# Thirty rows for every score and maxima product, with zero rows under the low parts, in a gated mix of local and full attention

## The chip, the core and the metric

The kernel runs on one core of one Trainium2 chip. The metric is the device time of one execution in microseconds (us); lower is better. The core has five engines that run side by side and wait for each other through semaphores: TensorE (PE; PEld is its weight load), VectorE (DVE), ScalarE (ACT), GpSimd (POOL) and SyncE (SP, which here issues nearly all DMAs).

## What is computed

For one sequence of S = 2048 positions with D = 448 features, 16 heads of 28 features each:

```python
x = A_x
g = _sigmoid((x * gate_w).sum(-1, keepdims=True))
a = _A_ref(x, A_wqkv, A_wo)   # each position looks at itself and 7 earlier ones, 2 apart
b = _B_ref(x, B_wqkv, B_wo)   # full attention over all positions, no mask
return g * a + (1 - g) * b
```

Both branches project x to queries, keys and values, take scores q.k times 28 ** -0.5, a softmax, the weighted sum of the values, and an output projection. All data are float32.

## The kernel before

**Precision.** A float32 operand is split into a high part, rounded to the format that TensorE takes in one pass (F32R), and a low part, the rest. A product of two such operands is the sum of three terms: high x high, high x low, low x high. The queries and keys of branch B go through DRAM as `qk_hi` and `qk_lo`.

**Tiles with four heads.** A key tile (`KH` high, `KL` low) has 128 rows: head h of a group of four sits in rows 32h to 32h+27. There are 4 such groups (g), and 4 blocks of 512 queries (b), so 16 units u = 4g + b. Rows 28 and 29 of each head have a special use in the first term: `KH` is filled with 1.0 before its keys are loaded (`init_kh`, L83), so these two rows stay 1.0, and rows 28 and 29 of the high query tile `QH` hold minus the row maximum of the scores, as a high and a low part (`load_nm`). So the first term, taken over 30 rows, yields the score minus the maximum. The two other terms take 28 rows.

**Projections (to about 248 us).** A list of tiles is worked through in order: the tiles of queries and keys of B, then values, then branch A. For each, TensorE multiplies (L320, L325), ScalarE, VectorE and GpSimd split and store. Between them TensorE already takes the first score maxima of B: `s1_mm` (L149) multiplies high queries (`QP`, two pairs of tiles in turn) and high keys, and VectorE reduces to the maximum (L171). In this part the maxima products take 64 rows, two heads at a time with the other one's query rows zero.

**Attention (from about 248 to 820 us).** 256 steps: for each unit, 16 key tiles of 128. In a step, `scores` issues 12 score products (4 heads x 3 terms, L1042) into three pairs of PSUM banks, and up to three maxima products for a later unit (L149, into T), in the order of the list `WITH` (`10 20 s0 11 21 30 00 ...`: head, then term; s for a maxima product), or `ALONE` when no maxima are left. Each product has 512 columns and stands in the row group of 32 rows of its head. ScalarE takes the exponential of two heads at once (L1047), VectorE the maxima (L155), and TensorE then multiplies the exponentials with the values (`av`, L1008). At the same time GpSimd and VectorE work through branch A from lists, with costs and due times that set which item is issued in which step. The query tiles of the next unit are loaded in step 12 of a unit (`load_q`, `load_part`): `QH` and `QL` come from a pool with two buffers each.

**End (from 820 us).** The output projection of both branches (L886).

**Fills.** At the start GpSimd fills `KH[0]` and `KH[1]` with 1.0 (L83), and VectorE fills a zero tile `t0` (L212) and two small ones. The third key tile `KH[2]` and the second low-key tile `KL[1]` get their memory when the projections' memory is free, in `main_tiles` in the first step of the attention stage; `KH[2]` is filled there, and then a mask (L620, L625). Keys are loaded later: into `KH[1]` behind tile 22, into `KL[0]` behind tile 62, into `KL[1]` in step 30. The order of instructions on each engine is the order in which the program issues them.

Of the kernel before, what the change touches and what calls it, by code (L numbers as in the profile page):

```python
# [8 lines left out]
F32 = mybir.dt.float32  # L9
F32R = mybir.dt.float32r  # L10
# [5 lines left out]
S, D, H, DH = 2048, 448, 16, 28  # L16
NB, NJ, NG = 4, 16, 4
W, DIL = 8, 2
HALO = (W - 1) * DIL
SCALE = DH ** -0.5  # L20
NU = NG * NB
NMX = 192
# [3 lines left out]
def gated_mix_kernel(ctx: ExitStack, tc: tile.TileContext, xT, xn, gw, wA, wB, woAB, out):  # L26
    nc = tc.nc
# [47 lines left out]

    QP = [[cp.tile([128, 512], F32R, name=f"QP{i}{k}") for k in range(2)] for i in range(2)]

    def init_kh(t):
        nc.gpsimd.memset(t.bitcast(F32), 1.0)  # L83

    def pair(name):
        return pp.tile([128, 2, 512], F32, tag="P", name=name)
# [18 lines left out]
            r = D + 112 * g + DH * h  # L105
            dma_r(t[32 * h:32 * h + DH, c], src[r:r + DH, c])

    def load_part(u, name, src):
        g, b = divmod(u, NB)
        t = sp.tile([128, 512], F32R, name=name)  # L110
        for h in range(4):
            r = 112 * g + DH * h
            dma_r(t[32 * h:32 * h + DH, :], src[r:r + DH, 512 * b:512 * b + 512])
        return t
# [1 line left out]
    Qs = {}  # L116

    def load_q(u, low=True):
        Qs[u] = load_part(u, "QH", qk_hi), load_part(u, "QL", qk_lo)
        if low:  # L120
            load_nm(u)

# [18 lines left out]
    def s1_mm(n, bank, half=False):  # L141
        u, i = divmod(n, 64)
        qs, kc, h = i // 16, i // 4 % 4, i % 4
        if u == 0:
            qs, kc = i // 8 % 4, 2 * (i // 32) + i // 4 % 2
        if i == 0 and u + 1 < NU:
            load_qhi(u + 1)
        r = slice(64 * (h // 2), 64 * (h // 2) + 64) if half else slice(32 * h, 32 * h + DH)
        nc.tensor.matmul(bank, qhis[u][h % 2][r, 128 * qs:128 * qs + 128],  # L149
                         KH[u // NB % 3][r, 512 * kc:512 * kc + 512], start=True, stop=True)  # L150

# [54 lines left out]
            nc.sync.dma_start(nm[u].bitcast(F32)[:, 32 * a:32 * a + 32], r[32 * a:32 * a + 32, :])  # L206


    for t in KH:
        init_kh(t)  # L210
    t0 = pair("t0")[:, 0, :]
    nc.vector.memset(t0, 0.0)  # L212
    nc.vector.memset(zt, 0.0)
    nc.vector.memset(omt, 0.0)

    zero = nc.const_aps.tensor(0.0, [128, 512], F32).bitcast(F32R)

# [8 lines left out]
    if True:  # L226
# [259 lines left out]
        for n, t in enumerate(tiles[:-1]):  # L486
            wi = t[0]
            for w in loads:
                if loads[w] == n:
                    load_w(w)  # L490
            for w in splits:
                i, k = (n - splits[w][0]) * splits[w][1], splits[w][1]
                if 0 <= i < 4:
                    split_w(w, range(i, i + k))
            if n in (3, 5):
                split_x((n + 1) // 2)
            if n < FULL:
                project(n)
            else:
                project_halves(n, [S1_START <= m < S1_START + 80 for m in (n, n + 1)])  # L500
            if n == 0:
                split_x(1, (3,))
            if t[1] == "qk":
                for m in {0: (), 1: (0, 1)}.get(n, (n,)):
                    qk_tile(m, *tiles[m][2:4])
            elif t[1] == "v":
                add_halves(n, V[:, t[2], :, 0:DH])
            else:
                a_tile(n, t[2], t[3])
            if n == 1:  # L510
                split_x(1, range(3))
            if n == 4:
                for t in QP[1]:
                    nc.scalar.activation(t, t0, AF.Copy)
            while fini and fini[0][0] <= n:
                fini.pop(0)[1]()
            if n == 2:
                load_w(1, (False,))
            if n == 3:
                load_qhi(0)  # L520
            if n in (3, 8):
                load_k(0, KH[0], qk_hi, slice(0, 1024) if n == 3 else slice(1024, S))
            if n == 3:
                load_w(1, (True,))
            if n == 16:
                for i in (1, 2):
                    nc.sync.dma_start(a_scr[i][:, 0:NJ, :].rearrange("c j e -> c (j e)").rearrange(
                        "c (a b) -> c a b", b=NJ), omg[0:8, None, :].to_broadcast([8, 56, NJ]))
            if n == 32:
                nc.gpsimd.memset(V[:, :, :, DH:], 1.0)  # L530
            if n == 22:
                load_k(1, KH[1], qk_hi)
            if n == 62:
                load_k(0, KL[0], qk_lo)
            if parts and parts[0][0] <= n:
                _, u, t = parts.pop(0)
                max_store(u, max_turn(t))
            if finished and n < len(tiles) - 3:
                u = finished.pop(0)
                parts.append((n + 3, u, max_parts(u)))  # L540
            if n == 64:
                gate = []
                for sgn, dst in ((-1.0, g_t), (1.0, omg)):
                    e = sp.tile([128, NJ], F32, name="ez")
                    nc.scalar.activation(e, zt, AF.Exp, scale=sgn)
                    nc.gpsimd.tensor_tensor(out=e, in0=e, in1=V[:, 0, :, DH], op=ALU.add)
                    gate.append((dst, e))
            if n in (66, 68):
                nc.vector.reciprocal(*gate.pop(0))
            if n == 70:  # L550
                r = sp.tile([128, 32], F32, name="omr")
                nc.vector.transpose(r, omt)
                for a in range(4):
                    nc.sync.dma_start(og_scr.rearrange("(j p) -> j p", j=NJ)[:, 32 * a:32 * a + 32],
                                      r[32 * a:32 * a + NJ, :])
            if n == 76:
                load_q(0)
# [51 lines left out]
    def main_tiles():  # L609
        nonlocal mp, pm, maskt, actx, a1, a2, a3  # L610
        hctx.close()
        mp = ctx.enter_context(tc.tile_pool(name="mp", bufs=1))

        KH.append(mp.tile([128, S], F32R, name="KH2"))
        KL.append(mp.tile([128, S], F32R, name="KL1"))
        init_kh(KH[2])
        pm = ctx.enter_context(tc.tile_pool(name="pm", bufs=8))

        maskt = mp.tile([128, W, NJ, 2], F32, name="maskt")
        nc.gpsimd.memset(maskt, 0.0)  # L620
        for st, g, t, src in ((12, 2, KH[2], qk_hi), (30, 1, KL[1], qk_lo), (72, 2, KL[0], qk_lo),
                              (100, 3, KH[0], qk_hi), (136, 3, KL[1], qk_lo)):
            at("end", st, lambda g=g, t=t, src=src: load_k(g, t, src))
        for w in range(1, W):
            nc.gpsimd.memset(maskt[0:1, w, 0:DIL * w, :], -1e9 / SCALE)  # L625

        actx = ExitStack()
        a1 = actx.enter_context(tc.tile_pool(name="a1", bufs=1))
        a2 = actx.enter_context(tc.tile_pool(name="a2", bufs=2))
        a3 = actx.enter_context(tc.tile_pool(name="a3", bufs=5))  # L630
        for nme in ("k", "v"):
            for i in range(2):
                t = a1.tile([128, HALO + NJ, 56], F32, name=f"{nme}t{i}")
                kvt[nme, i] = t
# [384 lines left out]
    def scores(u, kt, cur):  # L1019
# [9 lines left out]
        for tok in WITH if k else ALONE:  # L1029
            if tok[0] == "s":  # L1030
                i = int(tok[1])
                if i < k:
                    s1_mm(n + i, bank[tok])
                if i == 0:
                    s1_max(n, 1, T1)
                elif i == 2 and k > 1:
                    s1_max(n + 1, k - 1, other[:, 0:k - 1, :])
                continue
            a, t = tok[0], int(tok[1])
            h = (int(a) + n) % 4  # L1040
            r = slice(32 * h, 32 * h + (DH + 2 if t == 0 else DH))
            nc.tensor.matmul(bank[a], (KH[g % 3], KH[g % 3], KL[g % 2])[t][r, ks], (qh, ql, qh)[t][r, :], start=(t == 0), stop=(t == 2))  # L1042
            if t == 2 and a in "20":
                if len(exps) < 5:
                    probs.append(pair("P"))
                p = probs[len(exps) % 5]
                e = nc.scalar.activation(p, one if a == "2" else mine, AF.Exp, scale=SCALE).ins  # L1047
                for o in exps[-5:-4]:
                    tc.declare_no_dep(e, o, query=mybir.DependencyQuery.ANY_SYNC,
                                      reason="PE has read what it wrote, and this one waits for PE")  # L1050
                for o in maxs[-4:]:
                    tc.declare_no_dep(e, o, reason="PE waited for it and the exponential waits for PE")
                exps.append(e)
                cur[(h + 3) % 4], cur[h] = p[:, 0, :], p[:, 1, :]
                yield len(cur)
# [86 lines left out]
```

## Time and profile before

| | us |
|---|---|
| median of 3 runs | 896.78 (896.74 to 896.83) |
| the profiled execution | 896.69 |
| its span, first to last instruction | 894.9 |
| TensorE busy | 890.2 |
| VectorE busy | 740.5 |
| ScalarE busy | 642.4 |
| GpSimd busy | 638.7 |

The span is the time between the first and the last instruction of the profiled execution; the execution's own time has some 1.8 us around it. A busy engine is one with an instruction in flight; products of TensorE are pipelined and their ends are modelled, so starts tell more than ends. In a group's line stand line, engine, operation, output and inputs, shape, count, the busy time in all, and the mean duration in ns; behind it, in brackets or behind a bar, is the idle time before and what ended it.

### The profile page before, as it was taken

What the parts mean: (1) busy time and instruction counts of PE and PEld (TensorE: products, weight loads), DVE (VectorE), ACT (ScalarE), POOL (GpSimd) and SP (SyncE); (2) the same over time, 40 slices, a digit from 0 to 9 for tenths busy, and PEclk for the clock granted to TensorE, in tenths of its full rate; (3) what the DMA queues carried; (4) which work ended last, traced back from release to release, by engine and by line L of the source; (5) the groups of instructions that cost most, each with busy time, mean ns of one, the idle gap of its engine ahead of it and who ended that gap; (6) DMA issues with size and microseconds to landing.
All of it is one profiled execution on the core that took longest, in us unless ns stands there. A gap on an engine that the chain in (4) does not pass through costs nothing.

```text
span 894.9 us, 20516 instructions
## 1 busy us (share of the span) xinstructions
PE 890.2 (99%) x8312; PEld 533.4 (60%) x8312; DVE 740.5 (83%) x962; ACT 642.4 (72%) x766; POOL 638.7 (71%) x505
## 2 busy tenths in 40 slices
PE   9999999999999999999999999999999999999998
PEld 7889999999954444444444444444444444434997
DVE  6688999999979999999999999999999999832220
ACT  7456434343378898898988989989888898897220
POOL 1499846464459789998999989999999799701000
PEclk9999999999999999999999999999999999999999
DMA  8886403454372241225225222533121322437781
GB/s 267 277 267 186 151 12 84 135 142 121 103 248 66 89 139 46 67 61 156 71 56 143 86 62 86 128 96 98 45 64 32 89 43 49 104 78 214 192 265 52
DMA packets 114038, 104.51 MB, mean 117 GB/s; under 512 B 75240, under 2 KB 82280, under 8 KB 113160
## 3 DMA queue, kind: packets, MB, share of 16 engines
q1 hardware_dynamic: 113512, 102.42, 40.7%
q8 instruction: 65, 1.06, 0.5%
q10 hardware_dynamic: 432, 0.79, 0.3%
q14 instruction: 29, 0.24, 0.1%
HBM read 62.20 MB, written 40.96 MB: 115 GB/s over the span
## 4 chain that ended last, share of the span: by engine, by line
PE 99%; ACT 0%; issue 0%; ACTq 0%
PE T L1042 31%; PE av L1008 28%; PE r L325 15%; PE r L320 8%; PE T L886 8%; PE r L149 4%; PE T L149 4%; PE r L220 0%; PE av L472 0%; ACT P L1047 0%; ACT res L895 0%; ACT onhi L943 0%; ACT L L679 0%; ACTq L943 0%
## 5 line engine op out<-in xcount | busy, mean ns | idle before, releaser
L1047 ACT ACTIVATE P<-T 128x1024 f32<-128x1024 f32 x512 | 496.8, 1023 | 59.6 <-PE T L1042 57.9
L155 DVE TENSOR_REDUCE MX<-T 128x1 f32<-128x512 f32 x470 | 442.5, 954 | 31.7 <-PE T L149 13.7
L1008 PE MATMUL av<-P,V 128*32 128x512 f32 x2048 | 272.7, 605 | 0.0
L1042 PEld LDWEIGHTS T<-QH,KH 30*128 30x128 f32 x1024 | 92.2, 181 | 229.1 <-ACT P L1047 196.5
L149 PE MATMUL T<-KH,QP 28*128 28x512 f32 x704 | 220.3, 456 | 0.1
L1042 PE MATMUL T<-QH,KH 30*128 30x512 f32 x1024 | 211.7, 489 | 0.2 <-ACT P L1047 0.2
L171 DVE TENSOR_REDUCE MX<-r 128x2 f32<-128x1024 f32 x160 | 192.9, 1221 | 20.1 <-PE r L149 16.3
L1042 PE MATMUL T<-QH,KL 28*128 28x512 f32 x1024 | 185.7, 393 | 0.0
L1042 PE MATMUL T<-QL,KH 28*128 28x512 f32 x1024 | 184.3, 392 | 0.0
L653 POOL TENSOR_TENSOR prod<-qt,kt 128x896 f32<-128x896 f32 x64 | 135.4, 2116 | 6.4 <-DMA kt<-a_scr 6.4
L397 ACT ACTIVATE raw<-r 128x896 f32<-128x896 f32 (+1 forms) x62 | 57.1, 921 | 94.5 <-PE r L325 91.9
L149 PE MATMUL r<-KH,QP 64*128 64x512 f32 x320 | 114.5, 391 | 0.0
L714 POOL TENSOR_TENSOR oat<-oat,prod 128x896 f32<-128x896 f32 x48 | 101.2, 2109 | 2.0
L149 PEld LDWEIGHTS T<-KH,QP 28*128 28x128 f32 x704 | 86.1, 181 | 26.7 <-ACT P L1047 17.7
L325 PE MATMUL r<-wh,xh 64*128 64x448 f32 (+1 forms) x504 | 99.6, 363 | 0.0
L709 POOL TENSOR_TENSOR prod<-vt,L 128x896 f32<-128x896 f32 x56 | 95.3, 1702 | 0.3
L398 POOL TENSOR_TENSOR ast<-raw 128x448 f32<-128x448 f32 x47 | 54.3, 1154 | 56.4 <-ACT raw L397 43.9
L1042 PEld LDWEIGHTS T<-QL,KH 28*128 28x128 f32 x1024 | 94.3, 185 | 0.0
L1042 PEld LDWEIGHTS T<-QH,KL 28*128 28x128 f32 x1024 | 93.3, 183 | 0.2
L1008 PEld LDWEIGHTS av<-P,V 128*32 128x32 f32 x2048 | 40.3, 107 | 77.9 <-issue 65.4
L325 PE MATMUL r<-wl,xh 64*128 64x448 f32 (+1 forms) x441 | 79.0, 365 | 0.0
L325 PEld LDWEIGHTS r<-wh,xh 64*128 64x128 f32 x504 | 77.9, 185 | 0.1
(122 smaller groups left out, 1138.8 us busy)
## 6 DMA issues: line engine op xcount, KB each, us to landing
a_scr<-ast SPq DMA_DIRECT2D x24, 448.0 KB
qk_hi<-qkh SPq DMA_DIRECT2D x24, 256.0 KB
qk_lo<-qkh SPq DMA_DIRECT2D x24, 256.0 KB
rbc<-rs SPq DMA_DIRECT2D x64, 64.0 KB
QP<-qk_hi SPq DMA_DIRECT2D x64, 56.0 KB
KL<-qk_lo SPq DMA_DIRECT2D x16, 224.0 KB
QH<-qk_hi SPq DMA_DIRECT2D x64, 56.0 KB
QL<-qk_lo SPq DMA_DIRECT2D x64, 56.0 KB
```

The lines of the kernel that those rows point to most:

```text
L149: nc.tensor.matmul(bank, qhis[u][h % 2][r, 128 * qs:128 * qs + 128], KH[u // NB % 3][r, 512 * kc:512 * kc + 512], start=True, stop=True)
L155: i = nc.vector.tensor_reduce(MX[:, n % NMX:n % NMX + k], bank, axis=X, op=ALU.max)
L171: nc.vector.tensor_reduce(m, PM[k], axis=X, op=ALU.max)
L320: nc.tensor.matmul(bank, ws[c][rows, k, t[4]:t[4] + 128], x, start=first, stop=last)
L325: nc.tensor.matmul(bank[:, 0:cols], x, ws[c][rows, k, 0:cols], start=first, stop=last)
L653: nc.gpsimd.tensor_tensor(out=p, in0=qt[c], in1=kvt["k", c % 2][:, HALO - DIL * w:HALO - DIL * w + NJ, :], op=ALU.mult)
L709: nc.gpsimd.tensor_tensor(out=dst.rearrange("p j (h d) -> p j h d", d=DH), in0=kvt["v", c % 2][:, HALO - DIL * w:HALO - DIL * w + NJ, :].r ...
L714: nc.gpsimd.tensor_tensor(out=ows[c % 2][:, :, 0:56] if w == W - 1 else oat[c], in0=oat[c], in1=oat[c, w], op=ALU.add)
L886: writes(bank, nc.tensor.matmul(bank[:, :D], src, wo[c][k], start=(first and k == ks[0] and i == 0), stop=(last and k == ks[-1] and i == 2)))
L1008: nc.tensor.matmul(av[32 * h:32 * h + 32, :], V[:, kt, 4 * g + h, :], tiles_[h], start=(kt == 0), stop=(kt == NJ - 1), skip_group_check=True)
L1042: nc.tensor.matmul(bank[a], (KH[g % 3], KH[g % 3], KL[g % 2])[t][r, ks], (qh, ql, qh)[t][r, :], start=(t == 0), stop=(t == 2))
L1047: e = nc.scalar.activation(p, one if a == "2" else mine, AF.Exp, scale=SCALE).ins
```

## The change

Every score product and every maxima product of the attention stage takes 30 rows. For this the low query tiles `QL` become two fixed tiles, filled with zeros by VectorE at the start, and used in turn; the low key tiles are filled with zeros before their keys are loaded. So rows 28 and 29 are zero in one of the two operands of the second and the third term, and zero in the queries of a maxima product. `KH[1]` is filled in the program behind the fifth entry of the tile list (n == 4) and no longer at the very start, and `KL[0]` with it, both by GpSimd; `KL[1]` is filled by GpSimd in `main_tiles`, behind `KH[2]` and ahead of the mask.

```diff
+ROWS = DH + 2
...
+    QL = [cp.tile([128, 512], F32R, name=f"QL{i}") for i in range(2)]
...
+    def init_kl(t):
+        nc.gpsimd.memset(t.bitcast(F32), 0.0)
...
-    def load_part(u, name, src):
+    def load_part(u, t, src):
         g, b = divmod(u, NB)
-        t = sp.tile([128, 512], F32R, name=name)
...
-        Qs[u] = load_part(u, "QH", qk_hi), load_part(u, "QL", qk_lo)
+        Qs[u] = load_part(u, sp.tile([128, 512], F32R, name="QH"), qk_hi), load_part(u, QL[u % 2], qk_lo)
...
-        r = slice(64 * (h // 2), 64 * (h // 2) + 64) if half else slice(32 * h, 32 * h + DH)
+        r = slice(64 * (h // 2), 64 * (h // 2) + 64) if half else slice(32 * h, 32 * h + ROWS)
...
-    for t in KH:
-        init_kh(t)
+    init_kh(KH[0])
     t0 = pair("t0")[:, 0, :]
     nc.vector.memset(t0, 0.0)
     nc.vector.memset(zt, 0.0)
     nc.vector.memset(omt, 0.0)
+    for t in QL:
+        nc.vector.memset(t.bitcast(F32), 0.0)
...
             if n == 4:
                 for t in QP[1]:
                     nc.scalar.activation(t, t0, AF.Copy)
+                init_kh(KH[1])
+                init_kl(KL[0])
...
         init_kh(KH[2])
+        init_kl(KL[1])
...
-            r = slice(32 * h, 32 * h + (DH + 2 if t == 0 else DH))
+            r = slice(32 * h, 32 * h + ROWS)
```

## The prediction

> **What bounds the kernel now.** I read the page first, for the engine that the end hangs on; then the table of windows, to split the span into stages; then single steps of the attention stage in order of time; then the two source lines whose products the change touches; last the start of the span and the start of the attention stage, where the fills stand.
>
> ```profile
> span 894.9 us, 20516 instructions
> PE 890.2 (99%) x8312; PEld 533.4 (60%) x8312; DVE 740.5 (83%) x962; ACT 642.4 (72%) x766; POOL 638.7 (71%) x505
> PE 99%; ACT 0%; issue 0%; ACTq 0%
> PE T L1042 31%; PE av L1008 28%; PE r L325 15%; PE r L320 8%; PE T L886 8%; PE r L149 4%; PE T L149 4%; PE r L220 0%; PE av L472 0%; ACT P L1047 0%; ACT res L895 0%; ACT onhi L943 0%; ACT L L679 0%; ACTq L943 0%
> ```
>
> ```profile
> core 0: us, PE busy (x) PEld busy (x) DVE busy (x) ACT busy (x) POOL busy (x), PEclk, DMA share, GB/s
> 248.00:820.00 572.00, 571.73 (x5822) 238.37 (x5820) 514.37 (x735) 511.12 (x572) 488.08 (x350) 1.00 0.34 92
> ```
>
> The chain that ended last is TensorE from end to end, and the products that the change widens (L1042, and L149 into T) are 35% of it. The attention stage fills about 572 of the 894.9 us. It is 256 steps (16 units of 16 key tiles), so a step is about 572 / 256 = 2.23 us. TensorE is busy in all of it at a granted clock of 1.00, with ScalarE (511.12) and VectorE (514.37) at 90%. Full busy does not yet mean that TensorE streams all the time, so I looked into two steps. The lines give start, duration, and how many products were merged.
>
> ```profile
> 382.86 0.50 PE L1042 MATMUL T<-QH,KH 30*128 30x512 f32 x2
> 382.87 0.50 PE L149 MATMUL T<-KH,QP 28*128 28x512 f32 x1
> 383.08 0.49 PE L1042 MATMUL T<-QH,KH 30*128 30x512 f32 x1
> 383.20 0.40 PE L1042 MATMUL T<-QL,KH 28*128 28x512 f32 x2
> 383.21 0.39 PE L1042 MATMUL T<-QH,KH 30*128 30x512 f32 x1
> 383.42 0.39 PE L1042 MATMUL T<-QL,KH 28*128 28x512 f32 x1
> 383.43 0.39 PE L1042 MATMUL T<-QH,KL 28*128 28x512 f32 x1
> 383.44 0.39 PE L1042 MATMUL T<-QL,KH 28*128 28x512 f32 x1
> 383.44 0.60 PE L1042 MATMUL T<-QH,KL 28*128 28x512 f32 x2
> 383.66 0.41 PE L149 MATMUL T<-KH,QP 28*128 28x512 f32 x2
> 384.00 1.06 PE L1008 MATMUL av<-P,V 128*32 128x512 f32 x8
> 385.00 0.50 PE L1042 MATMUL T<-QH,KH 30*128 30x512 f32 x2
> ...
> 385.39 0.50 PE L1042 MATMUL T<-QH,KH 30*128 30x512 f32 x2
> 385.56 0.40 PE L1042 MATMUL T<-QH,KL 28*128 28x512 f32 x2
> ...
> 387.30 0.50 PE L1042 MATMUL T<-QH,KH 30*128 30x512 f32 x2
> ```
>
> A step holds 15 products of 512 columns in four row groups of 32, one for each head, which run side by side; so in one row group there are at most four in a row. In a row group the products follow each other every 0.23 us (383.20 to 383.43, 383.21 to 383.44). The first of a step takes 0.11 more, because its weight load is not hidden: 382.86 to 383.20 is 0.34. The first of these two steps takes 2.14 us (382.86 to 385.00), the second 2.30 (385.00 to 387.30); in the second the last two high products start only at 385.39, with the long duration, because their PSUM pair was still being read. So TensorE streams back to back but for such waits of about a tenth of a step. Whatever a wider product costs in streaming would show in the time in full; whatever only shortens a wait gains a few tenths of a microsecond in a step at most.
>
> **Part 1: rows 28 to 30.** Two of the three terms of a score (2 x 1,024 products) and the maxima products of this stage (704) get two more rows; that is 2,752 instructions and none more than before. Two more zero rows leave the sums as they are. The price is that of two rows in a product of 512 columns.
>
> ```profile
> engine op xcount: duration ns min/median/max, first and last start us, forms
> L1042 PE MATMUL T<-QH,KH x1024: 387/494/503, 248.4 to 819.5; 30*128 30x512 f32 x171
> L1042 PE MATMUL T<-QL,KH x1024: 384/392/417, 248.8 to 819.8; 28*128 28x512 f32 x171
> L1042 PE MATMUL T<-QH,KL x1024: 382/392/498, 249.0 to 820.1; 28*128 28x512 f32 x171
> L149 PE MATMUL T<-KH,QP x704: 382/489/505, 248.5 to 778.0; 28*128 28x512 f32 x176
> L149 PE MATMUL r<-KH,QP x320: 385/392/398, 32.0 to 245.5; 64*128 64x512 f32 x160
> ```
>
> These are minimum, median and longest duration in ns. At first sight 30 rows cost 494 and 28 rows 392. But the maxima products have 28 rows and a median of 489, and 64 rows take 392. The two values are a product whose weight load is hidden (382 to 398) and one whose load is not (about 490), in every shape. Which of the two it is hangs on what the product waited for: the 30-row product at 383.21 followed a 28-row one in its row group and took 0.39, the 28-row ones at 382.87 and 30-row ones at 382.86 opened a step and took 0.50 alike.
>
> Now the ends. The shortest 30-row product, 387, is 3 to 5 ns above the shortest 28-row ones, 384 and 382. Four run side by side, so 2,752 products are 688 in sequence, and 688 x 3 to 5 ns is 2.1 to 3.4 us more. The other end is the 64-row form against the longest of the hidden 28-row medians: 392 against 392 is 0, and from the shortest 64-row one, 385, to the 387 of 30 rows it is 2 ns less for more rows, 688 x 2 ns = 1.4 us less. I take 0: the distance between starts is the price in a stream, and it is 0.23 us behind a 30-row product (383.21 to 383.44) as behind a 28-row one (383.20 to 383.43).
>
> No new wait comes with the two rows. The second term reads rows of the key tile that the first term of the same head has read already; the third term reads the query rows with the maxima, which the first term of that head has waited for. The low query tiles stay two in turn, as they were in their pool, and their loads keep the same 28 rows, size and place in SyncE's queue.
>
> **Part 2: the fills.** At the start VectorE gets two fills of 128x512, GpSimd keeps the fills of the first two key tiles and gets one of 128x2048 for the low keys.
>
> ```profile
> 1.25 3.54 POOL L83 MEMSET KH<- 128x2048 f32 x2
> 30.26 1.03 POOL L235 TENSOR_TENSOR wl<-raw,wh 128x384 fp32r<-128x384 f32 x1 [25.47 <-ACT wh L234]
> 0.91 0.48 DVE L212 MEMSET t<- 128x512 f32 x1 [0.91 <-PEq L1134]
> 4.64 0.43 DVE L443 CAST xh<-V 128x512 fp32r<-128x512 f32 x1 [3.18 <-DMA V<-in_xT]
> 5.22 0.71 PE L320 MATMUL r<-xh,wh 128*128 128x512 f32 x2
> L862 DVE CAST oahi<-oar 128x512 fp32r<-128x512 f32 x3 | 1.3, 429 | 10.8 <-DMA oar<-oa_scr 10.8
> ```
>
> VectorE: 2 x 0.48 = 0.96 us, in the 3.18 us in which it waits for the first input; cost 0, and up to 0.96 if that cover were gone. GpSimd: in its own order there is nothing between the first key fill and the place behind four tiles, and the new fills wait for nothing, so I expect all three one behind the other at the start, ending near 4.79 + 1.8 = 6.6 us. The next thing GpSimd does is at 30.26, after 25.47 us of waiting. The first loads into those tiles are issued behind tile 22 and tile 62, long after. Cost 0; even if the fills were to wait for the fourth tile they would fit into the same gap.
>
> At the start of the attention stage GpSimd gets one more fill, for the second low-key tile, behind that of the third key tile.
>
> ```profile
> 252.50 1.81 POOL L83 MEMSET KH<- 128x2048 f32 x1 [1.86 <-PE av L472]
> 254.24 0.31 POOL L620 MEMSET maskt<- 128x256 f32 x1
> 254.95 0.21 POOL L192 TENSOR_TENSOR nmt<-nmv,nmt 128x16 fp32r<-128x16 f32 x1
> 261.60 2.13 POOL L653 TENSOR_TENSOR prod<-qt,kt 128x896 f32<-128x896 f32 x1 [6.44 <-DMA kt<-a_scr]
> 259.25 0.20 DVE L201 STREAM_TRANSPOSE nms<-nmt 128x32 f32<-128x32 f32 x1
> ```
>
> It takes 254.24 - 252.50 = 1.74 us of GpSimd's order. Behind it stand the mask fills and the low part of the maxima, which goes from 254.95 to about 256.7; VectorE's transpose of it starts at 259.25, still 2.3 us later. The first product waits for a load until 261.60 and keeps 6.44 - 1.74 = 4.7 us of slack. Cost 0; without that cover 1.74 us on GpSimd, which stands nowhere in the chain. The load of that tile, at step 30, is 30 x 2.23 = 67 us away.
>
> **The sum.** 0 + 0 + 0 against the profiled execution's 896.69 us (span 894.9 and 1.8 around it), which is 0.09 below the median of 896.78. Forecast: 896.8 us, no change that can be told: about 0.2%, or 1.8 us, is what a measurement of this kernel can tell from none.
>
> **Rivals.** *Slower: a lock at the start.* If the third fill holds VectorE off, the cast at 4.64 starts when that fill ends: 4.79 + 1.74 = 6.53, so 1.89 us later, and the first real products at 5.22 wait for that cast. TensorE has no slack to give it back: 898.7. It decides if the fill gets in before the cast, that is if the first input lands after about 4.73. Against it: the cast began 0.15 us before the second fill ended and took 0.43, as the casts of the same shape in line L862 took 0.429 on average; but 0.15 is little overlap, and GpSimd's ends are rough. [...]
>
> *Slower: two rows cost streaming time.* With the 3 to 5 ns above: 898.9 to 900.2. With the whole difference of the medians, 102 ns in 688, 70 us: 967, against which the 28-row products at 0.50 and the 30-row one at 0.39 speak outright.
>
> *Faster: mixed row counts were what kept weight loads from hiding.* Then the late pair of the 385.00 step would lose its 0.11 us, and with it every step: 256 x 0.11 = 28 us, 868.6. For it: most 30-row products have the long duration. Against it: low query products always follow a 30-row product in their row group, and their longest is 417; the maxima products at the end of a step follow a 28-row one, and more than half have the long duration.
>
> *It does not do what it says:* the fills run at the start and not behind four tiles, as said in part 2; that changes nothing in the sum.
>
> **How the numbers follow.** No change on the path: 0.77. Lock at the start: 0.07; streaming price of two rows: 0.08; faster by hidden loads or a better fit of the waits: 0.08. So faster 0.08, same 0.77, slower 0.15. The range goes down to the lower end of part 1 (896.8 - 1.4 = 895.4) and up to the first end of the streaming price (898.9), which takes in the lock; left out are the 28 us gain and the rest of the slow cases.
>
> **What the profile after would show.** Right: all T products of L1042 and L149 as 30x512, with shortest durations of 382 to 387 and 0.23 us from one to the next in a row group; steps of 2.14 to 2.30 us; three fills at the start, GpSimd's next work still near 30.3; the cast of L443 at 4.6 and the first real product at 5.2; GpSimd's first product still waiting for its load near 261.6. Wrong: a cast that starts at 6.5; a 0.24 us distance in a row group; low query products with durations near 490; a stage of attention that is more than 2 us longer or shorter than 572.

## The result, and the profile after

| | before | after |
|---|---|---|
| median of 16 runs, us | 896.81 | 898.61 |
| lowest to highest, us | 896.40 to 897.81 | 897.12 to 899.79 |
| the profiled execution, us | 896.69 | 898.69 |
| its span, us | 894.9 | 896.9 |

The ratio is 1.0015, with a 95% interval of 1.0008 to 1.0022: slower, by 1.3 us by the ratio and 1.8 by the medians, clear of no change at all and just about at the 0.2% up to which the prediction spoke of none. The result lies inside the stated range (895.4 to 898.9). But the three zeros of the sum are not what happened: the start cost about 3 us in the profiled execution and the attention stage gave 0.9 back. The runs after also spread more than those before, in three groups: five near 897.2, ten near 898.6 and one at 899.8.

The start of the changed kernel in order of time, VectorE, GpSimd, then TensorE (start, duration, what, in brackets the idle time before and what ended it):

```profile
1.52 1.02 DVE L219 MEMSET QL<- 128x512 f32 x2
4.65 2.17 DVE L448 CAST xh<-V 128x512 fp32r<-128x512 f32 x1 [2.11 <-DMA V<-in_xT]
6.86 0.69 DVE L453 TENSOR_TENSOR xl<-V,xh 128x512 fp32r<-128x512 f32 x1
...
1.25 3.55 POOL L85 MEMSET KH<- 128x2048 f32 x2
4.74 1.81 POOL L88 MEMSET KL<- 128x2048 f32 x1
...
6.97 0.70 PE L325 MATMUL r<-xh,wh 128*128 128x512 f32 x2 [1.69 <-DVE xh L448]
7.60 0.74 PE L325 MATMUL r<-xl,wh 128*128 128x512 f32 x2
8.18 0.81 PE L325 MATMUL r<-xh,wl 128*128 128x512 f32 x2
8.78 1.06 PE L325 MATMUL r<-xh,wh 128*128 128x512 f32 x2
9.64 1.06 PE L325 MATMUL r<-xl,wh 128*128 128x512 f32 x2
```

The first cast starts where it did (4.65, before 4.64) but takes 2.17 us in place of 0.43. It ends at 6.82, 0.28 us behind the end of the new fill at 6.55. The first real products wait for it until 6.97, before 5.22: 1.75 us later. Then comes something that stands in no rival: from about 8.8 us on, a pair of products takes 1.06 us, where it took 0.63. The table of windows has the granted clock beside it, in the column behind the busy times. The first two lines are after, the third is the last stretch before.

```profile
5.05:8.45 3.40, 1.71 (x7) 1.01 (x7) 3.37 (x5) 2.14 (x5) 1.49 (x1) 1.00 0.94 265
8.45:11.90 3.45, 3.45 (x10) 2.71 (x9) 3.35 (x9) 1.80 (x5) 0.00 (x0) 0.51 0.86 287
...
8.45:11.90 3.45, 3.45 (x16) 2.69 (x16) 2.10 (x5) 1.77 (x6) 0.00 (x0) 1.00 0.89 282
```

In the 3.40 us that hold the hole, TensorE was busy for 1.71; in the 3.45 us behind it the granted clock was 0.51, and it got through 10 products (before, at 1.00, 16).

Now the source line of the scores, after (minimum, median, longest in ns, then first and last start):

```profile
L1050 PE MATMUL T<-QH,KH x1024: 382/493/520, 251.3 to 821.5; 30*128 30x512 f32 x171
L1050 PE MATMUL T<-QL,KH x1024: 382/388/402, 251.7 to 821.8; 30*128 30x512 f32 x171
L1050 PE MATMUL T<-QH,KL x1024: 382/392/498, 251.9 to 822.1; 30*128 30x512 f32 x171
```

The first score product comes at 251.3 (before 248.4), so the start cost 2.9 us. The last comes 570.2 us later (before 571.1): the stage is 0.9 us shorter. The low query products (second term) have a median of 388 ns, before 392, though they have two rows more. The third term has two rows more as well, and keeps its 392.

### The profile page after: what moved, and what is told of

It reads as the page before. It is cut to its first block, busy times and chain, and to the rows that moved or that the text cites. A ratio compares the mean times of both kernels' runs of the same rounds, so it can differ in the third digit from the quotient of the medians.

```text
span 896.9 us, 20520 instructions
## 1 busy us (share of the span) xinstructions
PE 890.6 (99%) x8312; PEld 532.1 (59%) x8312; DVE 742.4 (83%) x964; ACT 642.6 (72%) x766; POOL 642.6 (72%) x507
## 3 DMA queue, kind: packets, MB, share of 16 engines
q8 instruction: 65, 1.06, 0.5%
## 4 chain that ended last, share of the span: by engine, by line
PE 98%; DMA 0%; ACT 0%; DVE 0%; issue 0%; ACTq 0%
PE T L1050 31%; PE av L1016 28%; PE r L330 15%; PE r L325 8%; PE T L894 8%; PE r L153 4%; PE T L153 4%; DMA V<-in_xT 0%; PE av L477 0%; ACT P L1055 0%; DVE xh L448 0%; ACT res L903 0%; ACT onhi L951 0%; ACT L L687 0%; ACTq L951 0%
## 5 line engine op out<-in xcount | busy, mean ns | idle before, releaser
L1055 ACT ACTIVATE P<-T 128x1024 f32<-128x1024 f32 x512 | 496.9, 1024 | 58.5 <-PE T L1050 56.4
L153 PE MATMUL T<-KH,QP 30*128 30x512 f32 x704 | 221.0, 458 | 0.1
L1050 PE MATMUL T<-QH,KL 30*128 30x512 f32 x1024 | 185.8, 394 | 0.0
L1050 PE MATMUL T<-QL,KH 30*128 30x512 f32 x1024 | 183.1, 388 | 0.0
L153 PEld LDWEIGHTS T<-KH,QP 30*128 30x128 f32 x704 | 86.0, 181 | 26.5 <-ACT P L1055 16.4
L1050 PEld LDWEIGHTS T<-QL,KH 30*128 30x128 f32 x1024 | 94.0, 184 | 0.0
L1050 PEld LDWEIGHTS T<-QH,KL 30*128 30x128 f32 x1024 | 92.8, 182 | 0.2
```

## The experiments

Two theories stood at first. A: the added fill of GpSimd holds VectorE's first cast, and TensorE's clock drops behind the hole; equal rows save 0.9 us. B: the cast is late for another reason, and the rows save nothing. All times are medians of 9 to 11 runs; the kernel before, on the same chips, had 896.63 to 896.72.

**The fill on another engine.**

```diff
-    for t in QL:
+    for t in QL + [KL[0]]:
         nc.vector.memset(t.bitcast(F32), 0.0)
...
-                init_kl(KL[0])
```

> The changed kernel with one edit: the first low-key tile is filled by VectorE at the start, behind the two low-query tiles (about 2 us more of fills, into its wait for the first input), and no longer by GpSimd; GpSimd has its two key fills as in the kernel before. Theory A (the added GpSimd fill holds the first cast of VectorE, 2.17 instead of 0.43 us, and TensorE's clock drops behind that hole; thirty rows everywhere save some 0.9 us in the attention stage): cast back at 0.43 us, first product near 5.2 us, no half clock at the start, 895.9 us, faster than both. Theory B (the cast is late through VectorE's own fills or the inputs' landing, and the rows save nothing): cast still long or late, 898 us or more.

Measured 895.82 us, ratio 0.9991 (0.9982 to 1.0000): 2.8 us under the change and 0.9 under the kernel before. The interval just reaches no change, but four more versions below lie at 895.87 to 896.00. VectorE's fill ends at 4.68, just as the input is there, and the cast is short again:

```profile
2.92 1.76 DVE L219 MEMSET KL<- 128x2048 f32 x1 [0.38 <-issue]
4.67 0.43 DVE L448 CAST xh<-V 128x512 fp32r<-128x512 f32 x1
```

The first products are at 5.24. B is out: VectorE has more fills of its own here than in the change, and the cast is not late.

**The fills alone, in the kernel before.**

```diff
-    for t in KH:
-        init_kh(t)
+    init_kh(KH[0])
...
+                init_kh(KH[1])
+                init_kl(KL[0])     # behind four tiles, GpSimd
```

> The kernel before with the GpSimd fills of the change alone: second key tile and first low-key tile filled behind four tiles in the program; rows, low-query tiles and all else as before. Theory A: the cast takes 2.1 to 2.2 us, the first product comes near 7.0, the attention stage (first to last step) stays at 571.0 us; 898.5 us where the clock holds, up to 900 where it drops behind the hole. Theory B: cast 0.43 us and 896.8 us.

Measured 899.40 us (897.75 to 900.61), ratio 1.0025 (1.0015 to 1.0034). The first products come at 6.97, and the mean granted clock of the profiled execution is 0.998, as in that of the change. VectorE's cast, GpSimd's fill, and the low query products of the scores:

```profile
4.62 2.20 DVE L445 CAST xh<-V 128x512 fp32r<-128x512 f32 x1 [3.16 <-DMA V<-in_xT]
...
4.74 1.81 POOL L86 MEMSET KL<- 128x2048 f32 x1
...
L1046 PE MATMUL T<-QL,KH x1024: 384/392/424, 251.6 to 822.5; 28*128 28x512 f32 x171
```

From the first to the last of them it is 570.9 us: the stage is as long as before (571.1), within 0.2. So the loss is all in the fills, 2.7 us, and the 0.8 us by which the change is better than this come from its other part.

**Another instruction in place of the cast.** The question is whether the hold strikes this one-input cast, or any instruction of VectorE that reads and writes in its place.

```diff
-        nc.vector.tensor_copy(xh[0][:, 0, :], r[:, 0, :])
+        nc.vector.tensor_tensor(out=xh[0][:, 0, :], in0=r[:, 0, :], in1=t0, op=ALU.add)
```

> The changed kernel with one edit: the first rounding of the input on VectorE is a sum of two tensors (the input and the zero tile) and no longer a one-input cast. [...] Theory A with a hold that strikes any VectorE instruction that reads and writes there: the sum takes 2.2 us or more, 898.6 us.

Measured 895.87 us (0.9991, 0.9982 to 1.0000), with the first products at 5.65. The fill is still where it was, and the sum runs beside it at its own speed:

```profile
4.82 0.69 DVE L448 TENSOR_TENSOR xh<-V,t 128x512 fp32r<-128x512 f32 x1 [2.28 <-DMA V<-in_xT]
...
4.73 1.81 POOL L88 MEMSET KL<- 128x2048 f32 x1
```

The sum of this shape takes 0.69 us with GpSimd idle too (at 5.13 in the run with the fill on VectorE, where GpSimd's fills end at 4.80). So reading and writing beside the fill do not hold VectorE by themselves: under the same fill of 1.81 us the one-input cast took 2.17 and the two-input sum 0.69. Why the one is held and the other is not, no run shows.

**A longer opening for TensorE.**

```diff
-    warm(10)
+    warm(14)
```

> The changed kernel with one edit: 14 opening products of zeros in place of 10, so that TensorE has work until about 6.9 us and the hole of 1.69 us ahead of the first real product is filled. Theory A: the cast still takes 2.17 us and the first product still comes near 7.0, but no stretch at half clock follows; 896.8 + 1.75 - 0.9 = 897.7 us in every execution. If the half clock costs nothing: 898.6 us as the changed kernel.

Measured 897.17 us (897.08 to 897.31). The cast still takes 2.04 us and the first products still start at 6.97, but with zero products in the hole the ones behind it take 0.62 to 0.63 us a pair from 8.18 on, and the granted clock from 8.45 to 11.90 is 1.00:

```profile
6.97 0.70 PE L325 MATMUL r<-xh,wh 128*128 128x512 f32 x2 [0.50 <-ACT wh L452]
7.60 0.73 PE L325 MATMUL r<-xl,wh 128*128 128x512 f32 x2
8.18 0.62 PE L325 MATMUL r<-xh,wl 128*128 128x512 f32 x2
8.63 0.62 PE L325 MATMUL r<-xh,wh 128*128 128x512 f32 x2
```

This splits the loss. Against 895.82 the held cast costs 1.35 us of the 1.75 by which the first product is late; and the hole with the drop of the clock behind it costs another 1.44 (898.61 - 897.17). From the clock an estimate is 1.7 us: 3.45 us at 0.51 lack 3.45 x 0.49. All 11 runs lie at 897.1 to 897.3, where 5 of the 16 runs of the change lie too, all five with a mean granted clock of 1.000; the profiled execution of the change, with the drop, is from the middle group. Of the ten runs of that group seven have a mean granted clock of 0.997 or 0.998; the other three have 1.000, and what slowed those is not shown. The expected 897.7 was 0.5 too high, since TensorE catches some up: in the kernel before its products stand up to 0.34 us apart between 13.41 and 16.11, here 0.23 or 0.24 all the way, and the lag falls from 1.75 to 1.32 (16.11 before; here an estimate of 17.43, from the start at 16.97 and two products at 0.23). Why they stand closer is not shown.

**The fill twice.**

```diff
                 init_kl(KL[0])
+                init_kl(KL[0])
```

> The changed kernel with the first low-key tile filled twice, one fill behind the other, so four fills of GpSimd in a row at the start. If the cast is held as long as GpSimd has fills in a row: it ends 0.28 us behind the fourth, 3.9 us long, first product near 8.7 us, 899.3 us where the clock holds and up to 901 where it drops. If a waiting cast gets its turn between two fills: 2.17 us as before, 898.6 us.

Measured 898.55 us (1.0020, 1.0011 to 1.0029), as the change. The cast is not held longer:

```profile
4.76 2.06 DVE L448 CAST xh<-V 128x512 fp32r<-128x512 f32 x1 [2.22 <-DMA V<-in_xT]
...
6.97 1.19 PE L325 MATMUL r<-xh,wh 128*128 128x512 f32 x2 [1.59 <-DVE xh L448]
7.96 1.05 PE L325 MATMUL r<-xl,wh 128*128 128x512 f32 x2
...
4.74 3.83 POOL L88 MEMSET KL<- 128x2048 f32 x2
```

Two fills take 3.83 us in a row, where the two of the key tiles take 3.55: 0.28 more, about what the held casts of the other runs have left behind the end of the fill. An estimate from that is that here the fourth fill waited 0.28 us for the cast. In this execution the first pair took 1.19 us already (0.70 in the change) and the next ones 1.05, up to about 13 us, though the clock column reads 1.00 there, from 5.05 to 11.90. The ten opening products took 4.60 us, in the change 4.50; there they start 0.43 us apart from the second on, as the pairs do here (0.85 to 0.86 for two), also at a clock of 1.00. What made the pairs slow no run shows. Its own time was 899.72 us, which is the highest group. What decides between the three groups is open.

**GpSimd idle when the cast comes.** On top of the first experiment:

```diff
-                init_kh(KH[1])
+            if n == 10:
+                init_kh(KH[1])
```

> The version with the low-key fill on VectorE (895.8 us), with the second key tile filled by GpSimd behind its first four instructions for the weights and one sum (at about 37 us) and no longer at the start, so that GpSimd is idle when the first cast comes. If the cast of the kernel before was held for a moment too (it started at 4.64 and ended 0.28 us behind GpSimd's second fill): its duration falls below 0.43 us, to some 0.3, and 895.7 us. If it was not: 0.43 us and 895.8 us, or some tenths more where the fill delays the sums near 37 us.

Measured 895.98 us (0.9992, 0.9983 to 1.0001): the same as 895.82, and the cast again takes 0.43 us:

```profile
4.67 0.43 DVE L448 CAST xh<-V 128x512 fp32r<-128x512 f32 x1
...
1.25 1.81 POOL L85 MEMSET KH<- 128x2048 f32 x1
...
37.32 1.82 POOL L85 MEMSET KH<- 128x2048 f32 x1
```

So the cast of the kernel before, 0.15 us of which lay under the second fill, lost nothing by it.

**Why equal rows are faster.** Two theories: U, a mix of row counts costs; R, 28 rows cost more than 30. All four kernels have the first experiment's edit; with that alone, 30 rows everywhere, it was 895.82 us and this line:

```profile
L1049 PE MATMUL T<-QL,KH x1024: 382/388/412, 248.6 to 819.0; 30*128 30x512 f32 x171
```

```diff
-ROWS = DH + 2
+ROWS = DH          # 28 everywhere
```

> The version with the low-key fill on VectorE (895.8 us), with 28 rows in every score and maxima product; it leaves out the two rows of the first term that subtract the row maximum. In the attention stage low query products took 392 ns at the median in the kernel before and 388 with thirty rows everywhere, and the stage got shorter by 0.9 us; open is why. Theory U (a mix of row counts costs): no mix here either, so 388 ns and 895.8 us. Theory R (28 rows themselves cost some 4 ns more than 30): 392 ns and 896.7 us.

```diff
-ROWS = DH + 2
+ROWS = 32          # and QH in two fixed, zeroed tiles
```

> The version with the low-key fill on VectorE (895.8 us), with 32 rows in every score and maxima product, the last two of them zero in the queries; the high query tiles are two fixed tiles for that, filled by ScalarE behind four tiles (1.1 us in its waits). Theory U: 388 ns and 895.8 us. Theory R: 388 ns or less if the price falls further with whole row groups; 895.8 us or some tenths less.

```diff
-        r = ... if half else slice(32 * h, 32 * h + ROWS)      # maxima
+        r = ... if half else slice(32 * h, 32 * h + DH)
```

> The version with the low-key fill on VectorE (895.8 us), with 30 rows in the scores and 28 in the maxima products of the attention stage. Theory U: in steps with maxima a mix stands in each, so most of the gain goes: 896.5 us, low query products near 392 ns. Theory R: only the 704 maxima products pay, a quarter of the 2,752: 896.0 us, low query products at 388 ns.

```diff
-            r = slice(32 * h, 32 * h + ROWS)                   # scores
+            r = slice(32 * h, 32 * h + (ROWS if t == 0 else DH))
```

> The version with the low-key fill on VectorE (895.8 us), with 30 rows in the maxima products and the first term, and 28 in the two other terms as in the kernel before. Theory U: the mix is as before, 896.7 us. Theory R: 2,048 of the 2,752 products pay, 896.5 us; low query products at 392 ns under both, maxima products shorter under R alone.

Measured, in this order: 895.90, 896.77, 896.00 and 896.51 us. The line of the low query products, in the same order (the last two numbers of the times are the first and last start, so their difference is the stage):

```profile
L1049 PE MATMUL T<-QL,KH x1024: 382/388/413, 248.7 to 818.8; 28*128 28x512 f32 x171
```

```profile
L1050 PE MATMUL T<-QL,KH x1024: 382/390/412, 249.1 to 819.6; 32*128 32x512 f32 x171
```

```profile
L1049 PE MATMUL T<-QL,KH x1024: 382/388/408, 249.1 to 819.3; 30*128 30x512 f32 x171
```

```profile
L1049 PE MATMUL T<-QL,KH x1024: 384/392/414, 248.7 to 819.6; 28*128 28x512 f32 x171
```

With 28 rows everywhere the gain is whole: R is out. With a mix among the three terms it is gone (392 ns, 570.9 us), with a mix between scores and maxima alone it is whole (388 ns, 570.2 us): U is right in a narrower form than I had put it, for the terms of a score. Between 895.9 and 896.5 us the step is small, but the median duration and the length of the stage go with it in these three runs and with 30 rows everywhere. Why a mix costs some 4 ns a low query product isn't shown. The 32 rows do not fit: without a mix U had 388 ns and 895.8 us, and they are in between (390 ns, 570.5 us) and 0.9 us slower in all. Whether that is the rows, the query tiles' new place or the two fills more on ScalarE is open, so U stands for 28 and 30 rows alone.

## Why the prediction was right, and where it was not

*The range held the result, the sum did not.* "0 + 0 + 0" was, by the runs: rows -0.9, held cast +1.35, hole and clock behind it +1.44 at the median, the fill at the attention stage 0. That is +1.9 where the forecast had nothing, and 1.8 were measured. It is luck in part that 898.61 lies inside the range: its upper end, 898.9, was the price of two rows in streaming, which did not come, and the clock stood in no term.

*Part 1, rows.* That the 102 ns between the medians are no price of rows held: after, the first term still has a median of 493 and the others 388 and 392, all at 30 rows. In the trace before, a high product of 0.50 us starts together with its weight load (both at 382.86), and a low query product of 0.40 us 0.23 us behind its own (383.20, load at 382.97); that the load is what takes the 102 ns no run tested. The zero was mis-sized: the stage got 0.9 us shorter. The 3 to 5 ns between the shortest products, from which the slower rival had its price, say nothing either way. The shortest first-term product is 387 ns in the kernel with 28 rows in the maxima alone, which has the gain, and 382 in the one with mixed terms, which has not:

```profile
L1049 PE MATMUL T<-QH,KH x1024: 387/493/520, 248.8 to 819.0; 30*128 30x512 f32 x171
L1049 PE MATMUL T<-QH,KH x1024: 382/494/503, 248.3 to 819.2; 30*128 30x512 f32 x171
```

What goes with the gain is the median of the low query products, 388 or 389 with it and 392 without; in all these runs the third term has 391 or 392 and the maxima 488 or 489. So an estimate of the gain is 1,024 low query products, four side by side, 256 x 4 ns = 1.0 us, near the 0.9 of the stage; the prediction's 688 products in sequence are too many. And a comparison of two shapes that run mixed can't give the price of either alone. The lower end of the range, 1.4 us, came from a wrong reason: the 64-row products are in another stage, in another mix.

*Part 2, fills at the start.* This is the step that failed. The place in GpSimd's queue, the start and the end (6.6) were right, and so was that nothing in the program waits for the fill; "cost 0" took GpSimd's idle time for cover and did not ask whether an instruction of another engine is held while the fill runs. The lock at the start was the rival with a chance of 0.07, and what I held against it was the cast's 0.15 us under the second fill: too little overlap to bear it, as I wrote and then did not act on. The held casts started at 4.62 to 4.78 and all ended at 6.82, 0.27 to 0.28 us behind the end of the fill. A free cast takes 0.43, so an estimate is that its first 0.15 us (0.43 - 0.28) ran ahead of the fill's end and the rest behind it. Then the cast under the second fill was no evidence against a lock, nor was the condition right that the first input has to land after 4.73: a cast that started at 4.65 was held. The sign that I had named for this rival, a cast that starts at 6.5, did not show either: the hold stands in the cast's length. Its price was 1.89 with nothing given back (the first product came 1.75 late, and 1.35 of that stayed), and it lacked a term: behind the hole of 1.69 us in TensorE's work the granted clock was 0.51 for 3.45 us, and with the hole filled the median was 1.44 less. That 898.7 and 898.61 agree is the sum of a loss too small by the clock and a gain left out.

*Part 2, VectorE's fills and the fill at the attention stage.* Right. VectorE's two fills took 1.02 us of its wait. GpSimd's order at the stage moved by 1.75 us against the third key tile's fill, and its first product still waited for its load:

```profile
255.38 1.81 POOL L85 MEMSET KH<- 128x2048 f32 x1 [1.87 <-PE av L477]
257.13 1.81 POOL L88 MEMSET KL<- 128x2048 f32 x1
...
264.63 2.11 POOL L661 TENSOR_TENSOR prod<-qt,kt 128x896 f32<-128x896 f32 x1 [4.82 <-DMA kt<-a_scr]
```

*It does not do what it says.* Right as a reading (the fills run at the start, not behind four tiles), wrong in "changes nothing": a fill that had really stood behind the tiles would not have met the cast at 4.65, as the second key tile's fill at 37.32 did not in the run with GpSimd idle.

*Faster by hidden loads.* Did not happen: as before, most first-term products have the long duration. One reading against this rival was off: of the 704 maxima products before, more than half have the long duration, but that counts the 234 or so that open a step; of the others about 200 of 470 have more than 440 ns, less than half.

## What to carry to other kernels

Idle time of an engine was not free cover here: GpSimd had waited 25.47 us in the place of the added fill of 1.81, and the fill still held a cast of VectorE on the path for 2.17 us in place of 0.43. So look for short instructions of other engines that are on the path while an added one runs, and read their durations after. Moving the one fill to VectorE's own wait, or the one cast to another form, turned +1.8 us into -0.9. And where a change opens a hole in TensorE's work, read the granted clock behind it (here 0.51 over 3.45 us) and try to fill it; here four more products of zeros saved 1.44 us at the median.

## What was not expected of the hardware

A one-input cast of VectorE under a GpSimd fill took 2.04 to 2.20 us in place of 0.43, even where its recorded start (4.65) lies 0.09 us before that of the fill (4.74); a two-input sum under the same fill took 0.69. With four fills in a row the cast was held for one of them, not two (one run). In the change, a stretch of 3.4 us in which TensorE was busy for half, with no idle time over 1.69 us, was followed by one of 3.4 us at a granted clock of 0.51; five of its 16 runs took 1.4 us less than the median, as the 11 with the hole filled, whose profiled execution had 1.00 in that stretch. And the second-term products of a score, of 512 columns, took 392 ns at the median where 28 and 30 rows are mixed among its terms, against 388 with either count alone.
